# A causal convolution and an RWKV channel mix on one core: dummy matmuls and mu's transpose ahead of the convolution

## Chip, cores and metric

One NeuronCore of a Trainium2 chip. The metric is the device time of one execution in microseconds (us); a median is over several executions. Some of the numbers come from one execution that was profiled.

## What is computed

`x` is 8 x 4160 x 192, in float32. A depthwise causal convolution with 7 taps runs along the sequence, with one softmaxed row of taps for each of 8 heads of 24 channels. Its result goes through a channel mix in the manner of RWKV, which blends each token with its predecessor by `mu_k` and `mu_r`:

```python
w = softmax(weight)                       # 8 x 7
y[b, s] = sum_k w[h, k] * x[b, s - 6 + k] # per channel, h is its head
y_prev  = y shifted by one token (zero ahead of the first)
xk = mu_k * y + (1 - mu_k) * y_prev
xr = mu_r * y + (1 - mu_r) * y_prev
k  = relu(xk @ w_k)                       # 192 -> 1024
v  = (k * k) @ w_v                        # 1024 -> 192
out = sigmoid(xr @ w_r) * v
```

## The kernel before

TensorE (PE in the profile) does the convolution as matmuls with banded 128 x 128 matrices (`toe`, one for each head), and then the three products. The batch is taken in four pairs; a pair's tokens are cut into groups for the convolution and into steps of 512 tokens (the first has 256) for the channel mix. A step is cut into slots, each of which fills one PSUM tile of 128 x 1024 with `ps_k`. A slot runs on PE (`k_mm`, L592), then through ReLU on ScalarE (`k_relu`, ACT, L604), then squared on VectorE (`k_square`, DVE, L618). Four slots make a bundle, and the order of all work is written out by hand: each engine runs its instructions strictly in the order of the program text (`tc.manual_schedule`), bundle by bundle, with tables that say which step's blend, convolution or output goes into which bundle.

The change is in what runs ahead of the first bundles. `prologue` (L825) does this:

- SP and ACT issue the loads of the taps and of group 0's `x` (`x_f`, in float32); SP then issues two small loads of `mu_raw` (L176), 1.5 KB each, the last ones on its queue for the next 25 us. POOL issues the load of group 1's `x` (`xb`), makes masks, and issues the loads of `w_k` in two halves (L225), then more of `x`, `w_r` and `w_v`.
- PE first runs dummies that nobody reads: `SHORT` = 85 matmuls of one column (L852), then `WARM[0]` = 3 of 512 columns (`warm`, L823). They need only `ones_t` and `zeros`. Then come, in `softmax` (L240), eight small matmuls that spread the taps over the partitions (L253); they wait for VectorE's `w_tap` (L251). Then `WARM[1]` = 2 more dummies of 512 columns, while VectorE builds `toe` from the taps (`make_toe`, L295) and ACT casts group 0's `x` (L246).

`bundle_first` (L870) then convolves groups 0 and 1, three blocks of 64 channels each. For a block, `conv_t` (L402, matmuls at L412) writes a PSUM tile, ACT casts it to `yT` (`to_yT`, L422), and for group 0 VectorE forms the difference of neighbours (`diff`, L535) and blends it (`mix`, L548) into `xk`. The blend needs `mu` as one value per partition: `turn_mu` (L281) transposes `mu_raw` on PE into the dummies' PSUM tile `warm_ps`, and VectorE copies it from there (L882). The transpose stands behind the first block of the convolution:

```python
for n, (g, c) in enumerate((g, c) for g in range(2) for c in range(NC)):
    o = tiles[n % 2][:, n // 2 % 2, :]
    conv_t(g, c, o, range(groups[g][2]))
    if n == 0:
        turn_mu()
    to_yT(g, c, o, 0, groups[g][2], nc.scalar.copy)
```

Group 0 has 3 blocks of time for each channel block, so 3 x 24 matmuls; group 1 has 4, so 3 x 32. Behind them `bundle_first` runs the four slots of step 0, with the blend of step 1 on VectorE beside them.

Of the kernel before, what the change touches and what calls it, by code (L numbers as in the profile page):

```python
# [14 lines left out]
def kernel(  # L15
# [11 lines left out]
    nc = tc.nc  # L27
# [5 lines left out]
    P = 128  # L33
# [13 lines left out]
    NPAIR = B // 2  # L47
    YC = 16
    WARM = (3, 2)
    SHORT = 85  # L50

    const = ctx.enter_context(tc.tile_pool(name="const", bufs=1))
    two = ctx.enter_context(tc.tile_pool(name="two", bufs=2))
# [25 lines left out]
    n = 0  # L79
# [34 lines left out]
    def x_tile(g):  # L114
        p, base, nb, _, on_pe = groups[g]
        first = g if g in sparse else (0, 4, 6)[(g > 3) + (g > 5)]
        if g == first:
            homes[g] = two.tile([P, TG, 2, D], BF16, tag="xb", name="xb")
        n0 = sum(grp[2] for grp in groups[first:g])
        xb = homes[first][:, n0 : n0 + nb, :, :]  # L120
        xbs[g] = xb
        if g > 4:

            nc.vector.memset(xb[0:1, 0, 0, 0:2], 0.0)  # L124
        if base == 0 and g > 0:
            nc.gpsimd.memset(xb[0:32, 0, :, :], 0.0)  # L126
        if on_pe is False and base + 2 * nb * HB > S:
            n0 = nb - (base + 2 * nb * HB - S) // HB - 1
            nc.gpsimd.memset(xb[Q:P, n0:nb, :, :], 0.0)

    def load_x(g, batches=range(2)):
        p, base, nb, _, on_pe = groups[g]
        xb = xbs[g]
        if on_pe:
            parts, step, rows = ((0, base),), BLK, P
        elif g in sparse:
            parts, step, rows = [(32 * i, base + i * nb * TB) for i in range(4)], TB, 32
        else:
            parts, step, rows = ((0, base), (Q, base + nb * HB)), HB, Q
        for s in batches:  # L140
            b = 2 * p + s
            for q0, start in parts:
                lo, hi = 0, nb
                t0 = start - HALO
                if t0 < 0:
                    lo = 1
                    nc.gpsimd.dma_start(out=xb[HALO:rows, 0, s, :], in_=x[b, 0 : rows - HALO, :])
                while t0 + (hi - 1) * step + HALO + step > S:
                    hi -= 1
                    r0 = t0 + hi * step  # L150
                    if r0 + HALO < S:
                        nc.gpsimd.dma_start(out=xb[q0 : q0 + S - r0, hi, s, :], in_=x[b, r0:S, :])
                nc.gpsimd.dma_start(  # L153
                    out=xb[q0 : q0 + rows, lo:hi, s, :],
                    in_=bass.AP(
                        tensor=x.tensor,
                        offset=x.offset + (b * S + t0 + lo * step) * D,
                        ap=[[D, rows], [step * D, hi - lo], [1, D]],
                    ),
                )  # L160

    def load_x_first(eng, q0, q1, n0, n1, s0, s1):

        rows = [[D, q1 - q0]]
        rest = [[BLK * D, n1 - n0]] if n1 - n0 > 1 else [[S * D, s1 - s0]]
        eng.dma_start(
            out=x_f32[q0:q1, n0:n1, s0, :] if n1 - n0 > 1 else x_f32[q0:q1, n0, s0:s1, :],
            in_=bass.AP(
                tensor=x.tensor,
                offset=x.offset + (s0 * S + n0 * BLK - HALO + q0) * D,  # L170
                ap=rows + rest + [[1, D]],
            ),
        )

    def load_mu(i, m):
        nc.sync.dma_start(  # L176
            out=mu_raw[i * NC : (i + 1) * NC, :].rearrange("c (s q) -> c s q", s=2),
            in_=bass.AP(tensor=m.tensor, offset=m.offset, ap=[[Q, NC], [0, 2], [1, Q]]),
        )

    place = three.tile([P, NF * STEP], FP32, tag="k2", name="x_f32")
    n = groups[0][2] * 2 * D
# [5 lines left out]
    zeros = const.tile([P, BANK], BF16)  # L188
    ones_t = const.tile([P, P], BF16)
# [9 lines left out]
    warm_ps = ring.tile([P, 2, BANK], FP32, tag="k", name="warm")  # L199
# [34 lines left out]
    def load_wr():  # L234
        load_thirds(wr, moe_w_r, D)
# [21 lines left out]
    def masks_tap():  # L257

        nc.gpsimd.affine_select(
            out=tap8.rearrange("p (c r) -> p c r", r=8),  # L260
            in_=ones_t[0:8, 0:8].unsqueeze(1).to_broadcast([8, P // 8 + 1, 8]),
            pattern=[[0, P // 8 + 1], [-1, 8]],
            compare_op=ALU.is_equal,
            fill=0.0,
            base=0,
            channel_multiplier=1,
        )

    def select_equal(t, n):
        nc.gpsimd.affine_select(  # L270
            out=t,
            in_=(ones_t if t is ident else ones6)[0:n, 0:n],
            pattern=[[1, n]],
            compare_op=ALU.is_equal,
            fill=0.0,
            base=0,
            channel_multiplier=-1,
        )

    def turn_mu():  # L280
        nc.tensor.transpose(out=warm_ps[:, 1, 0 : 2 * NC], in_=mu_raw, identity=ident6)  # L281

    def masks_band():
        nc.gpsimd.affine_select(
            out=band, in_=ones_t, pattern=[[-1, P]], compare_op=ALU.is_ge, fill=0.0, base=0, channel_multiplier=1
        )
        nc.gpsimd.affine_select(
            out=band, in_=band, pattern=[[1, P]], compare_op=ALU.is_ge, fill=0.0, base=K - 1, channel_multiplier=-1
        )

    def make_toe():

        for h0, h1 in ((0, 3), (3, 6), (6, H)):
            n = h1 - h0
            nc.vector.tensor_tensor(  # L295
                out=toe[:, h0:h1, :].rearrange("p h (c r) -> p h c r", r=8),
                in0=w_per[:, h0:h1, :].unsqueeze(2).to_broadcast([P, n, P // 8, 8]),
                in1=band.rearrange("p (c r) -> p c r", r=8).unsqueeze(1).to_broadcast([P, n, P // 8, 8]),
                op=ALU.mult,
            )  # L300
# [520 lines left out]
    def warm(ps, n):  # L821
        for i in range(n):
            nc.tensor.matmul(out=ps[:, i % 2, :], lhsT=ones_t, rhs=zeros, start=True, stop=True)  # L823

    def prologue():  # L825
        nc.sync.dma_start(
            out=w_raw,
            in_=weight,
        )
        nc.vector.memset(x_f32[0:32, 0, :, :], 0.0)  # L830
        nc.vector.memset(ones_t, 1.0)
        for st, eng in ((0, nc.scalar), (1, nc.sync)):
            load_x_first(eng, 0, P, 1, groups[0][2], st, st + 1)
        load_x_first(nc.scalar, 16, P, 0, 1, 0, 2)
        load_x_first(nc.sync, HALO, 16, 0, 1, 0, 2)
        load_mu(0, moe_mu_k)
        load_mu(1, moe_mu_r)
        nc.scalar.preload_act_table(AF.Exp)
        nc.vector.memset(zeros, 0.0)
        nc.vector.memset(w_nrm, 0.0)  # L840
        nc.vector.memset(ones6, 1.0)
        x_tile(0)
        x_tile(1)
        load_x(1)
        masks_tap()
        select_equal(ident6, 2 * NC)
        masks_band()
        load_wk(0, DF // 2)

        for i in range(SHORT):  # L850
            q = slice(i % 4 * 32, i % 4 * 32 + 32)
            nc.tensor.matmul(  # L852
                out=warm_ps[q, 0, 0:1], lhsT=ones_t[:, 0:32], rhs=ones_t[:, 0:1], start=True, stop=True
            )
        warm(warm_ps, WARM[0])
        x_tile(2)
        softmax()
        warm(warm_ps, WARM[1])
        make_toe()
        load_wk(DF // 2, DF)  # L860
        load_x(2)
        select_equal(ident, P)
        x_tile(3)
        load_x(3)
        load_wr()
        load_wv()
        x_tile(4)
        load_x(4)

    def bundle_first(ns):  # L870
        new_yT(0)
        tiles = [ring.tile([P, 2, BANK], FP32, tag="k", name="ps_t") for _ in range(2)]
        for n, (g, c) in enumerate((g, c) for g in range(2) for c in range(NC)):
            o = tiles[n % 2][:, n // 2 % 2, :]
            conv_t(g, c, o, range(groups[g][2]))
            if n == 0:
                turn_mu()
            to_yT(g, c, o, 0, groups[g][2], nc.scalar.copy)
            if g == 0:
                diff(0, slice(c, c + 1))  # L880
                if c == 0:
                    nc.vector.tensor_copy(out=mu.rearrange("p i c -> p (i c)"), in_=warm_ps[:, 1, 0 : 2 * NC])  # L882
                mix(0, 0, slice(c, c + 1))

        diff(1, slice(0, 1))
        mix(1, 0, slice(0, 1))
        for n in ns[:2]:
            k_mm(n)
            k_relu(n)
        diff(1, slice(1, 3))  # L890
        scale(1, 0, 1, 2)
        add_y(1, 0, slice(1, 3))
        for n in ns[2:]:
            k_mm(n)
            k_relu(n)
        for n in ns:
            k_square(n)
        run(late, 0)
# [166 lines left out]
```

## Time and profile before

| | us |
|---|---|
| median of three timed runs | 411.61 |
| lowest, highest of them | 411.23, 412.36 |
| the profiled execution | 410.53 |
| its span, first to last instruction | 408.80 |
| busy in the span: PE, VectorE, ScalarE, POOL | 400.9, 370.9, 354.6, 57.6 |
| convolution's first matmul (L412) | 5.56 after the span's start |
| mu's transpose (L281) | 6.29 |
| first matmul of the channel mix (L592) | 10.12 |
| first ReLU (L604) | 11.69 |

The span is what the profile shows; the time of the execution has 1.73 us around it. PE and PEld are TensorE's matmuls and weight loads, which overlap. The page states for groups of instructions how long one takes and what ended the idle time before it; the timeline lists the instructions in order, merged where they follow one another. Times of the early stage are counted from the start of the span.

### The profile page before, as it was taken

How to read it: one execution, taken by the hardware profiler on the slowest of the kernel's cores; microseconds unless marked ns; L12 is line 12 of the kernel's file. 1: busy time of each engine (PE TensorE's matmuls, PEld its weight loads, DVE VectorE, ACT ScalarE, POOL GpSimd, SP SyncE). 2: the span in 40 equal slices, each digit the busy share in tenths (PEclk: the TensorE clock that was granted, in tenths of full speed). 3: DMA queues.
4: the chain of work that ended last, by engine and by line, in shares of the span. 5: the costliest groups of instructions: out<-in, count | busy, mean ns of one | idle time of the engine just before them, and what ended most of it. 6: DMA issues, size and time to landing. Idle time of an engine off the chain costs nothing.

```text
span 408.8 us, 17415 instructions
## 1 busy us (share of the span) xinstructions
PE 400.9 (98%) x7670; PEld 302.1 (74%) x7670; DVE 370.9 (91%) x672; ACT 354.6 (87%) x426; POOL 57.6 (14%) x91
## 2 busy tenths in 40 slices
PE   7899999999999999999999999999999999999996
PEld 4567767777867777777777777777777778777795
DVE  5999899998989999989999899999999899999973
ACT  6899988898998889988898998889899877877781
POOL 8732022030060004004020022000000000000000
PEclk9999999999999999999999999999999999999999
DMA  9999889996779978989995997977523856221223
GB/s 150 185 200 227 181 182 219 240 203 181 152 109 221 238 201 128 218 219 180 197 167 128 217 196 128 165 190 199 127 79 92 197 145 159 79 73 48 80 79 117
DMA packets 139124, 66.35 MB, mean 162 GB/s; under 512 B 89365, under 2 KB 139049, under 8 KB 139049
## 3 DMA queue, kind: packets, MB, share of 16 engines
q1 hardware_dynamic: 95704, 48.32, 46.8%
q0 software_dynamic: 42544, 16.36, 34.6%
q8 instruction: 60, 0.98, 1.0%
q10 hardware_dynamic: 800, 0.57, 0.5%
q14 instruction: 16, 0.12, 0.1%
HBM read 33.29 MB, written 36.99 MB: 172 GB/s over the span
## 4 chain that ended last, share of the span: by engine, by line
PE 91%; DMA 1%; SPq 1%; ACT 1%; issue 0%; DVE 0%; ACTq 0%
PE ps_v L680 40%; PE ps_k L592 39%; PE ps_r L649 8%; PE ps_c L363 2%; PE ps_v L632 1%; DMA y_dram<-y 1%; PE ps_c L318 1%; SPq L465 1%; ACT k_sb L604 1%; ACT y L336 0%; ACT y L438 0%; PE ps_c L392 0%; DVE o_sb L716 0%; ACTq L400 0%; ACTq L336 0%
## 5 line engine op out<-in xcount | busy, mean ns | idle before, releaser
L604 ACT ACTIVATE k_sb<-ps_k 128x1024 bf16<-128x1024 f32 x260 | 253.3, 1038 | 33.5 <-PE ps_k L592 32.8
L618 DVE TENSOR_TENSOR k<-k_sb 128x1024 bf16<-128x1024 bf16 x260 | 173.3, 686 | 25.4 <-ACT k_sb L604 25.3
L592 PE MATMUL ps_k<-xk,wk 64*128 64x512 bf16 (+1 forms) x1632 | 191.9, 367 | 1.2 <-DMA wk<-in_moe_w_k_dram 1.1
L680 PE MATMUL ps_v<-wv,k 64*128 64x192 bf16 x4032 | 188.4, 243 | 0.1
L680 PEld LDWEIGHTS <-k 64*128 64x128 bf16 x4032 | 168.4, 94 | 12.5 <-issue 4.8
L592 PEld LDWEIGHTS <-wk 64*128 64x128 bf16 x1632 | 83.3, 94 | 56.7 <-DMA wk<-in_moe_w_k_dram 1.6
L153 POOL DMA_DIRECT2D xb<-in_x_dram x62 | 44.0, 717 | 142.1 <-DVE xb L124 58.9
L696 DVE TENSOR_TENSOR o_sb<-ps_v,r_sb 128x768 f32<-128x768 f32 x64 | 60.8, 950 | 2.6 <-issue 2.4
L660 ACT ACTIVATE r_sb<-ps_r 128x768 bf16<-128x768 f32 x65 | 53.6, 827 | 8.7 <-PE ps_v L680 7.2
L336 ACT CAST y<-ps_c 128x960 bf16<-128x960 f32 (+2 forms) x84 | 52.7, 707 | 0.2 <-DMA y_dram<-y 0.2
L649 PEld LDWEIGHTS <-xr 64*128 64x128 bf16 x780 | 34.9, 94 | 14.1
L649 PE MATMUL ps_r<-wr,xr 64*128 64x192 bf16 x780 | 43.2, 243 | 0.0
L566 DVE TENSOR_SCALAR xr<-d,mu 128x512 bf16<-128x512 bf16 (+1 forms) x102 | 35.0, 347 | 0.0
L566 DVE TENSOR_SCALAR xk<-d,mu 128x512 bf16<-128x512 bf16 (+1 forms) x99 | 32.8, 360 | 0.1
L535 DVE TENSOR_TENSOR d<-yT 128x1536 bf16<-128x1536 bf16 (+4 forms) x36 | 31.2, 868 | 1.0 <-ACT yT L422 0.8
L572 DVE TENSOR_TENSOR xr<-xr,yT 128x1536 bf16<-128x1536 bf16 (+1 forms) x33 | 31.1, 941 | 1.1
L572 DVE TENSOR_TENSOR xk<-xk,yT 128x1536 bf16<-128x1536 bf16 (+3 forms) x33 | 30.4, 922 | 0.1
L519 POOL COPY y_tail<-yT 128x195 bf16<-128x195 bf16 x4 | 2.7, 673 | 90.2 <-DMA yT<-y_dram 90.2
L363 PEld LDWEIGHTS <-toe 32*32 32x32 bf16 x640 | 4.4, 87 | 8.6 <-issue 7.4
L363 PE MATMUL ps_c<-xb,toe 32*32 32x240 bf16 x640 | 9.3, 267 | 0.0
L126 POOL MEMSET xb<- 32x384 bf16 x3 | 1.2, 408 | 55.3 <-DVE xb L124 55.3
L412 PEld LDWEIGHTS <-xb 128*32 128x32 bf16 (+3 forms) x264 | 4.4, 104 | 2.7 <-issue 1.3
(58 smaller groups left out, 65.1 us busy)
## 6 DMA issues: line engine op xcount, KB each, us to landing
out_dram<-o_sb SPq DMA_DIRECT2D x128, 192.0 KB
xb<-in_x_dram POOLq DMA_DIRECT2D x52, 240.0 KB, 8.1
y_dram<-y SPq DMA_DIRECT2D x40, 195.0 KB
y_dram<-y SPq DMA_DIRECT2D x16, 210.0 KB
xb<-in_x_dram POOLq DMA_DIRECT2D x4, 228.0 KB, 4.5
xb<-in_x_dram POOLq DMA_DIRECT2D x4, 192.0 KB, 6.7
wk<-in_moe_w_k_dram POOLq DMA_DIRECT2D x4, 192.0 KB, 6.1
xb<-in_x_dram POOLq DMA_DIRECT2D x2, 216.0 KB, 5.2
```

Of the source, the lines that this page charges most:

```text
L153: nc.gpsimd.dma_start(out=xb[q0 : q0 + rows, lo:hi, s, :], in_=bass.AP(tensor=x.tensor, offset=x.offset + (b * S + t0 + lo * step) * D, ap ...
L336: nc.scalar.copy(out=bass.AP(tensor=y.tensor, offset=y.offset + d, ap=[y.ap[0], [m * 2 * D, 2], [2 * D, m], [Q, 2], [1, b - a]],), in_=bas ...
L535: nc.vector.tensor_tensor(out=shaped(s, diffs[s][:, cs, :L]), in0=y_of(s, cs, 1), in1=y_of(s, cs, 0), op=ALU.subtract)
L566: nc.vector.tensor_scalar(out=t[:, c, :L], in0=diffs[s][:, c, :L], scalar1=mu[:, i, c : c + 1], scalar2=None, op0=ALU.mult)
L572: nc.vector.tensor_tensor(out=o, in0=o, in1=y_of(s, sl, 0), op=ALU.add)
L592: nc.tensor.matmul(out=ps[:, i, f * L : (f + 1) * L], lhsT=wk[r, c, fs], rhs=xk[r, c, :L], start=c == 0 and f == 0, stop=c == NC - 1 and f ...
L604: nc.scalar.activation(out=k_sb, in_=ps.rearrange("p a b -> p (a b)"), func=AF.Relu)
L618: nc.vector.tensor_tensor(out=o, in0=i, in1=i, op=ALU.mult)
L649: nc.tensor.matmul(out=ps[:, i, k * D : (k + 1) * D], lhsT=xr[q, c, ts], rhs=wr[q, c, :], start=c == 0, stop=c == NC - 1,)
L660: nc.scalar.activation(out=r_sbs[s, j], in_=r_ps.pop((s, j))[:, :, 0 : 2 * D], func=AF.Sigmoid)
L680: nc.tensor.matmul(out=v_ps[s, j][:, bank, k * D : (k + 1) * D], lhsT=k2s[s][q, f, t * P : (t + 1) * P], rhs=wv[q, f, :], start=half == 0 ...
L696: nc.vector.tensor_tensor(out=o_sb.rearrange("p (b t) d -> p b (t d)", b=2), in0=v_ps.pop((s, j)), in1=r_sbs.pop((s, j)), op=ALU.mult,)
```

## The change

A new helper `fill` issues dummy matmuls of 128 columns into the first bank of `warm_ps`. Six of them follow the first three long dummies, in front of the tap matmuls. `turn_mu` moves out of `bundle_first` to behind the last two long dummies, in front of the whole convolution, and three more short fills follow it. Nine one-column dummies are dropped, so that PE has as many instructions as before.

```diff
     WARM = (3, 2)
-    SHORT = 85
+    SHORT = 76
+    FILL = (6, 3)
...
+    def fill(n):
+        for i in range(n):
+            nc.tensor.matmul(out=warm_ps[:, 0, 0:P], lhsT=ones_t, rhs=zeros[:, 0:P], start=True, stop=True)
+
     def prologue():
...
         warm(warm_ps, WARM[0])
+        fill(FILL[0])
         x_tile(2)
         softmax()
         warm(warm_ps, WARM[1])
+        turn_mu()
+        fill(FILL[1])
         make_toe()
...
             conv_t(g, c, o, range(groups[g][2]))
-            if n == 0:
-                turn_mu()
             to_yT(g, c, o, 0, groups[g][2], nc.scalar.copy)
```

## The prediction

> **What bounds the kernel now.** I read the page first, then the chain of waits, then the first 16 us in order of time, because the diff touches nothing later. The page gives PE 98% of the span. From about 29 us to the end the chain of waits is PE work with hardly a gap, so whatever moves the end must move PE's start into that stretch. The question is whether anything ahead of the convolution (L412) does so. The timeline, whose columns are start, duration, engine, line, operation, and in brackets the idle time ahead of it with its releaser:
>
> ```profile
> 3.98 0.20 DVE L251 STREAM_TRANSPOSE w_tap<-w_nrm 32x32 bf16<-32x32 bf16 x1
> 4.23 0.36 PE L253 MATMUL w_ps<-w_tap,tap 8*128 8x8 bf16 x8 [0.48 <-DVE w_tap L251]
> 4.53 1.03 PE L823 MATMUL warm<-zeros,ones_t 128*128 128x512 bf16 x2
> 5.56 0.79 PE L412 MATMUL ps_t<-toe,xb 128*32 128x120 bf16 x24
> 6.29 0.27 PE L281 MATMUL warm<-ident,mu_raw 6*128 6x6 f32 x1
> 6.41 0.46 ACT L422 CAST yT<-ps_t 128x360 bf16<-128x360 f32 x1
> 6.48 1.64 PE L412 MATMUL ps_t<-toe,xb 128*32 128x120 bf16 x50
> ...
> 8.34 1.02 PE L412 MATMUL ps_t<-toe,xb 128*32 128x120 bf16 x62 [0.22 <-DMA xb<-in_x_dram]
> ...
> 8.96 0.48 DVE L548 SCALAR_TENSOR_TENSOR xk<-d,mu,yT 128x256 bf16<-128x256 bf16 x1
> ...
> 10.12 0.28 PE L592 MATMUL ps_k<-xk,wk 64*128 64x256 bf16 x1
> ...
> 10.83 1.48 PE L592 MATMUL ps_k<-xk,wk 64*128 64x256 bf16 x24 [0.43 <-DMA wk<-in_moe_w_k_dram]
> ...
> 12.36 0.69 DVE L572 TENSOR_TENSOR xk<-xk,yT 128x1024 bf16<-128x1024 bf16 x1
> ...
> 13.01 2.77 PE L592 MATMUL ps_k<-xk,wk 64*128 64x256 bf16 x35 [0.69 <-DMA wk<-in_moe_w_k_dram]
> ...
> 14.93 0.69 DVE L618 TENSOR_TENSOR k<-k_sb 128x1024 bf16<-128x1024 bf16 x1 [0.57 <-ACT k_sb L604]
> ...
> 15.84 0.69 DVE L618 TENSOR_TENSOR k<-k_sb 128x1024 bf16<-128x1024 bf16 x1 [0.22 <-ACT k_sb L604]
> ```
>
> Three transfers pace the start: PE reaches group 1 of the convolution and waits for xb until 8.34, reaches the first FFN slot at 10.12 and waits for wk until 10.83, and waits for wk's second half until 13.01. All are issued by POOL, which waits for nothing that PE does here. Behind wk, ACT's ReLUs run from 11.69 to 18.66 with one hole of 0.24 us. So PE work that ends sooner before 10 us ends in front of a closed door.
>
> The matmul durations, as minimum, median, maximum in ns with first and last start, show the clock, which the page's PEclk row (nines throughout) does not; and the mu transpose has a semaphore wait of its own on PE's queue:
>
> ```profile
> L412 PE MATMUL ps_t<-toe,xb x264: 213/216/308, 5.6 to 17.9; 128*32 128x120 bf16 x67, 128*16 128x120 bf16 x24, 128*24 128x120 bf16 x23, 128*8 128x120 bf16 x18
> ```
>
> ```profile
> L281 PEldq EVENT_SEMAPHORE  x1: 51/51/51, 6.2 to 6.2; - x1
> L281 PE MATMUL warm<-ident,mu_raw x1: 266/266/266, 6.3 to 6.3; 6*128 6x6 f32 x1
> ```
>
> One by one in the trace, the matmuls of L412 take 279 to 308 ns and four go out per 100 ns up to 7.57; from 8.34 they take 216 ns at four per 52.5 ns. The clock doubled between 7.84 and 8.34 us.
>
> [...] the trace's 512-column dummies start 427 ns apart (2.697 and 3.124)[...]. [...]
>
> **Part by part.**
> *Nine short dummies fewer.* The 85 go out from 1.535 to 2.195, 7.9 ns apart: 9 x 7.9 = 0.07 us earlier for the long dummies. Nothing waits for those but PE itself, which then waits for w_tap: 0.
> *fill(6).* Cold, 128 columns are a quarter of 427, 107 ns: 6 x 107 = 0.64 us, from 3.48 (3.55 less 0.07) to 4.12. w_tap ends at 4.18 and the tap matmuls start at 4.23. It fits, with 0.1 us to spare; bounds 0 and, if a dummy drags its weight load (0.1 us each at most), +0.5 on the taps, which toe passes on. I take 0. [...]
> *turn_mu moved.* It issues no DMA and passes no queue but PE's. It takes 0.20 us of PE (6.287 to the next start, 6.483), 0 net since it only moves. But it waits for mu_raw. The completion marks of the mu_r load, read in the trace's raw records, are at 5.46, 5.62 and 6.12, and the transpose starts 0.17 us after the last; the convolution's matmul before it started at 6.05. So today the transpose is already held by that load, by about 0.1 us. Moved ahead, it stands in PE's queue from about 5.0 (warm) or 5.3 (cold), and all of the convolution is queued behind it; ACT's casts of ps_t (L422) wait for that, and VectorE for them. If mu lands as before: transpose at 6.29, fill(3) from 6.48 (3 x 107 = 0.32 cold; at half, 0.16 warm), convolution at 6.64 warm or 6.80 cold instead of 5.56. If mu lands by 5.3 the delay is only 0.20 + 0.16 to 0.32 less the present gap of 0.2: 0.15 to 0.3. I take the late landing.
> *Where the delay goes.* Group 0 has 72 matmuls. Warm at 13.1 ns: 6.64 + 0.95 = 7.6, ahead of the 7.67 of today. Cold at 25 ns with the switch at 8.1: 52 by then, 20 more by 8.36. Both meet xb at 8.34. VectorE's chain for xk of step 0 ends at 9.44 today. Its head, the first L412 third, ends later by 1.24 cold and by 1.24 − 0.16 (fills) − 24 x 12 ns (0.29, the first third at full clock) = 0.8 warm. So xk is whole at 10.2 warm or 10.7 cold, and its last third is needed at about 11.2, after wk's 10.83: hidden, by 0.5 at least. VectorE had 0.13 idle before the next step, so it is 0.67 warm or 1.1 cold late there: xk of step 1 at 13.7 or 14.2 instead of 13.05; PE needs it after 12 pairs of 0.109 from 13.01, 14.3: hidden, by 0.1 in the cold case. Then the two idle times before L618, 0.57 + 0.22 = 0.79, take the rest: 0 warm, 0.3 cold.
> *Sum.* 0 warm; cold up to +0.3, of which VectorE's later holes take some more. Without the cover of wk the warm case would cost 0.7. Against the profiled execution, 410.53 (span 408.80 plus 1.73 around it), that is 410.53 to 410.8. The median of the three timed runs is 1.08 higher, so I predict 411.61 + 0 = **411.6**.
>
> **The rivals.**
> *A: the usual execution starts colder than the profiled one, and the change mends that.* For it: [...] 410.53 lies below all three timed runs (411.23 to 412.36). If the switch came only after slots 0 and 1, their 12 pairs would take about 0.107 more each, 1.28 us; ACT's one hole of 0.24 takes little of it, so 1.0 to 1.3 reach ReLU's unbroken row. Ended in all executions: 411.61 − 1.3 = 410.3. [...]
> *B: slower, by mu's wait.* The hole from 5.3 to 6.29, 1.0 us of idle array, is larger than the one that fill(6) closes[...]. [...] group 0 ends at 8.6 and group 1 (96 x 25 ns) at 11.0; the FFN's first slots run cold: 0.2 of late start and 12 pairs x 0.107 = 1.28, less 0.24, give +1.25, so 412.9. It decides from the point where the clock comes after about 12 us[...]. For it: the completion mark at 6.12. [...]
> *C: the fills bring no clock at all but mu's wait is short.* Then everything is as today, at 411.6 to 411.9; it ends inside the forecast's own bound.
>
> **How the numbers follow.** A measurement of this kernel can tell about 0.3% (1.23 us) from no change, so "same" is 410.38 to 412.84. The forecast with C: 0.58, all same, 411.3 to 411.9 but for scatter of some 0.4 between medians (the three runs span 1.1). A: 0.26, most of it under 410.4; B: 0.16, at 412.1 to 412.9 or beyond, most of it over. I put faster 0.24, same 0.62, slower 0.14. The range takes in A's 410.3 and goes toward B: 410.3 to 412.7.
>
> **What would show it.** L412's durations at 216 ns from the first on, and 128-column dummies 54 ns apart in the second pause, show the early clock; 308 ns up to 8 us or later refute it. The transpose of L281 starting at about 6.3 with PE idle from 5.0 on shows mu's wait; a start near 5.2 refutes it. xb at 8.34 and wk at 10.83 and 13.0 unchanged, with the first ReLU at 11.7, show that the transfers cover it all. The prediction is wrong if wk's transfers land earlier or later than now, if the ReLU row starts later than 11.9, or if the timed executions differ from the profiled one by their clock.

## The result and the profile after

The changed kernel takes 416.28 us (median of 6 runs, 415.09 to 417.34) against 411.42 for the kernel before (6 runs, 410.10 to 412.52): ratio 1.0113, 95% interval 1.0087 to 1.0140. It is slower by 4.9 us. The profiled execution took 416.32 us, with a span of 414.6.

The timeline of the changed kernel's PE from 6 us on; all lines of code stand a little lower (L282 is the transpose, L413 the convolution, L593 the first product, L828 the fill):

```profile
6.21 0.24 PE L282 MATMUL warm<-ident,mu_raw 6*128 6x6 f32 x1 [0.61 <-DMA mu_raw<-in_moe_mu_r_dram]
6.38 0.50 PE L828 MATMUL warm<-zeros,ones_t 128*128 128x128 bf16 x3
6.81 3.38 PE L413 MATMUL ps_t<-toe,xb 128*32 128x120 bf16 x123
13.33 1.33 PE L413 MATMUL ps_t<-toe,xb 128*32 128x120 bf16 x45 [3.15 <-issue]
14.59 1.68 PE L593 MATMUL ps_k<-xk,wk 64*128 64x256 bf16 x14
```

The mu wait is there, as forecast, and the convolution starts at 6.81 instead of 5.56. What the prediction didn't have is the fourth line: PE stops in the middle of a block of group 1, after 123 of its 168 matmuls, and stands still for 3.15 us with the releaser "issue", which means that the profile shows nothing that it waited for. Its waits up to 30 us say it again (us in total, times, longest):

```profile
PE ps_t L413 <- issue: 3.1, 1, 3.1
...
PE warm L282 <- DMA mu_raw<-in_moe_mu_r_dram: 0.6, 1, 0.6
```

What came meanwhile is in the DMA view. The queues of the kernel before, from 4 to 6 us (packets, MB, share of the 16 engines, which passes 100% where the times of packets overlap):

```profile
q0 software_dynamic: 713, 0.27, 122.3%
q8 instruction: 1, 0.02, 2.9%
q1 hardware_dynamic: 32, 0.01, 2.4%
q10 hardware_dynamic: 11, 0.01, 0.9%
```

The same stretch of the changed kernel, and then its 10 to 13.3 us:

```profile
q0 software_dynamic: 765, 0.29, 126.3%
q1 hardware_dynamic: 65, 0.03, 5.9%
q10 hardware_dynamic: 55, 0.03, 5.4%
```

```profile
q0 software_dynamic: 1121, 0.61, 136.3%
q8 instruction: 1, 0.02, 1.8%
```

The page gives q8 and q14 the kind "instruction". It has these rows for the whole of the kernel before, and q8's counts are the same in the changed one:

```profile
q8 instruction: 60, 0.98, 1.0%
q14 instruction: 16, 0.12, 0.1%
```

PE has 7,670 matmuls and as many weight loads on the page, and 0.98 MB over 15,340 is 64 bytes for each; the other engines together run some 2,000 instructions, which at that size fits q14's 0.12 MB. By these counts q8 carries PE's instructions: each of its 60 packets is 16 KB in the trace's records, at 64 bytes 256 instructions. **The first of them starts at 4.91 us in the kernel before and at 11.06 in the changed one.** In the trace PE had started 448 instructions (444 weight loads and matmuls, two at its start and two waits for semaphores) when it stopped at 9.94, and it went on at 13.33, 2.27 us after the packet's start. In the kernel before, with the packet at 4.91, PE started its 449th instruction at 8.93 without such a stop.

**Where the 5.8 us of the two profiled spans lie.** The 123rd matmul of the convolution starts 0.97 us later than before (9.94 against 8.98): mu's wait and a cold clock. Then PE stands from 9.94 to 13.33, 3.39 us. The remaining stretches to the first ReLU take 0.05 longer in sum, so that the ReLU row starts at 16.09 instead of 11.69, 4.40 later. Instruction for instruction, PE is 4.21 us behind at 27 us and stays there up to 119 us. By 134 us it is 4.75, by 210 us 5.86, and 5.81 at the end; the last large step is one more stop without a visible reason:

```profile
208.98 0.31 PE L364 MATMUL ps_c<-xb,toe 32*32 32x240 bf16 x11 [0.87 <-issue]
```

Here, too, a q8 packet started 2.6 us before (206.40). One such stop also stands in the profile of a kernel below that loses nothing in all (a_short79, at 243.8 us, with its packet 2.2 us before), which suggests that the later ones belong to the scatter of this kernel and not to the change; that isn't shown.

The clock follows the stop: behind it the trace's clock record has half speed from 13.39 to 16.81 us, and matmuls of L413 take up to 308 ns again. Before 10 us the changed kernel's matmuls of L413 took 279 to 308 ns in 118 of 123 cases, so cold (73 of the first 123 in the kernel before), and the clock record has the first grant of full speed at 9.98, when PE had just stopped. Three stretches of 1 us of the changed kernel follow, each with its length, the busy time of PE, PEld, VectorE, ScalarE and POOL with their instructions, then the granted clock, the DMA share and GB/s; the clock goes from 1.00 to 0.50:

```profile
13.00:14.00 1.00, 0.67 (x32) 0.67 (x35) 0.00 (x0) 0.10 (x1) 0.23 (x2) 0.70 1.58 189
14.00:15.00 1.00, 1.00 (x31) 0.68 (x24) 0.00 (x0) 0.76 (x2) 0.84 (x2) 0.50 1.59 188
15.00:16.00 1.00, 1.00 (x12) 0.76 (x10) 0.69 (x1) 0.25 (x1) 0.71 (x2) 0.50 1.60 191
```

### The profile page after: what moved, and what is told of

It is laid out like the page before. It is cut to its first block, busy times and chain, and to the rows that moved or that the text cites. A ratio compares the mean times of both kernels' runs of the same rounds, so it can differ in the third digit from the quotient of the medians.

```text
span 414.6 us, 17414 instructions
## 1 busy us (share of the span) xinstructions
PE 403.4 (97%) x7669; PEld 305.0 (74%) x7670; DVE 370.6 (89%) x672; ACT 354.8 (86%) x426; POOL 57.2 (14%) x91
## 4 chain that ended last, share of the span: by engine, by line
PE 92%; ACT 1%; issue 1%; DVE 0%; ACTq 0%
PE ps_v L681 41%; PE ps_k L593 39%; PE ps_r L650 8%; PE ps_c L364 2%; PE ps_v L633 1%; PE ps_c L319 1%; ACT k_sb L605 1%; ACT y L439 0%; PE ps_c L393 0%; DVE o_sb L717 0%; ACTq L401 0%; ACTq L605 0%
## 5 line engine op out<-in xcount | busy, mean ns | idle before, releaser
L593 PE MATMUL ps_k<-xk,wk 64*128 64x512 bf16 (+1 forms) x1632 | 192.5, 368 | 0.3 <-ACT k_sb L605 0.3
L593 PEld LDWEIGHTS <-wk 64*128 64x128 bf16 x1632 | 84.3, 95 | 55.4 <-issue 1.3
L413 PE MATMUL ps_t<-toe,xb 128*32 128x120 bf16 (+3 forms) x264 | 6.3, 271 | 3.1 <-issue 3.1
```

Source lines behind the costliest of these rows:

```text
L593: nc.tensor.matmul(out=ps[:, i, f * L : (f + 1) * L], lhsT=wk[r, c, fs], rhs=xk[r, c, :L], start=c == 0 and f == 0, stop=c == NC - 1 and f ...
```

## The experiments

The first theory, F, a guess: PE asks for its next block of instructions on passing a certain instruction; mu's wait holds it short of that, and the request then queues behind POOL's loads. The rival, M: mu's wait and the cold clock cost the time by themselves. In what follows "fetch" is the start of the first 16 KB packet on q8, from one profiled execution of each kernel; the medians are over all runs. Instructions are counted in PE's own program, a weight load and a matmul being two.

### Three dummies more, and the parts alone

```diff
-    SHORT = 76
+    SHORT = 79          # a_short79: the changed kernel
...
-    SHORT = 85
+    SHORT = 76          # b_short76: the kernel before
```

> The changed kernel with three more one-column dummies (79), so that six more PE instructions stand ahead of mu's transpose, 196 instead of 190; all else is as changed. Theory F (instruction fetch: PE asks for its next block of instructions on passing about instruction 192 to 197; in the changed kernel it stands at number 191, waiting for mu, until 6.2 us, and then the fetch queues behind POOL's loads until 11): the first 16 KB fetch goes out near 5 us as before, no stall of PE inside group 1 of the convolution, 411 to 412 us. Theory M (mu's wait and the cold clock cost the time by themselves): mu still waits until 6.2, so 416 us as changed.

> The kernel before with 76 one-column dummies instead of 85 and nothing else: no fills, mu's transpose in its old place. Theory F: 18 instructions fewer stand ahead of the convolution, so the same instruction number is passed only after the convolution's start at 5.5 us, about 0.8 us later than before; the first fetch then comes behind POOL's loads, at 8 us or later, and if after 9 PE stalls in group 1: 412 to 416 us. Theory M: no difference, 411.4 us.

```diff
         warm(warm_ps, WARM[1])
-        turn_mu()
         fill(FILL[1])       # a_mu_back: the changed kernel
...
             conv_t(g, c, o, range(groups[g][2]))
+            if n == 0:
+                turn_mu()
```

> The changed kernel with mu's transpose put back behind the convolution's first block; the nine fills and the 76 short dummies stay. Theory F: nothing holds PE ahead of instruction 197, as in the kernel before; first fetch near 5 us, no stall, 411 to 412 us. Theory M: mu's wait is gone too, so the same, 411 to 412 us. A theory that the fills themselves cost the time: 415 us or more.

```diff
+        load_mu(0, moe_mu_k)
+        load_mu(1, moe_mu_r)
         nc.vector.memset(x_f32[0:32, 0, :, :], 0.0)   # a_mu_first: the changed kernel
...
         load_x_first(nc.sync, HALO, 16, 0, 1, 0, 2)
-        load_mu(0, moe_mu_k)
-        load_mu(1, moe_mu_r)
```

> The changed kernel with SP's two loads of mu issued straight after the taps' load, ahead of the loads of x; the transpose stays ahead of the convolution. Mu should land by 4 us, so that the transpose waits for nothing. Theory F: first fetch near 5 us, no stall; 411 to 412 us, or 411.0 if the fills bring the clock early. Theory M: mu's wait is gone, 411 to 412 us as well. If it stays at 416, both are wrong and the place of the transpose or the fills cost the time in another way.

| | median us | ratio to before, interval | fetch, us |
|---|---|---|---|
| a_short79 | 411.32 | 0.9995 (0.9981 to 1.0008) | 4.98 |
| b_short76 | 411.03 | 0.9990 (0.9976 to 1.0004) | 6.74 |
| a_mu_back | 411.61 | 1.0006 (0.9983 to 1.0029) | 6.42 |
| a_mu_first | 412.12 | 1.0004 (0.9989 to 1.0020) | 7.55 |

Three one-column dummies, 24 ns of PE at 7.9 ns from one to the next, take the whole loss away, while mu's wait stays. The waits of a_short79 up to 30 us:

```profile
...
PE ps_k L593 <- DMA wk<-in_moe_w_k_dram: 1.3, 1, 1.3
PE ps_t L413 <- DMA xb<-in_x_dram: 0.5, 1, 0.5
PE ps_t L413 <- ACT yT L423: 0.5, 2, 0.2
PE warm L282 <- DMA mu_raw<-in_moe_mu_r_dram: 0.2, 1, 0.2
```

There is no "issue" on PE; the longest are for transfers, as in the kernel before. That speaks against M, and a_short94 below, which has mu's wait and a cold clock as long as the changed kernel's, refutes it. F is in trouble too: b_short76, which by F should ask late and lose, loses nothing, and in a_mu_back and a_mu_first the fetch comes at 6.42 and 7.55 us and not near 5. Each part alone is free in time; the loss needs both.

### How sharp the step is

`SHORT = 77` and `SHORT = 78` in the changed kernel, and, for the pair without any fill, the kernel before with `SHORT = 76` and `turn_mu()` moved to behind `warm(warm_ps, WARM[1])`:

> The changed kernel with one more short dummy: 192 PE instructions ahead of mu's transpose. Theory F, now with a place: the request falls at one instruction between the 191st (the changed kernel, which is held there) and the 196th (79 short dummies, which is not). If at the 192nd or earlier, fetch near 5 us and 411.4; if later, fetch behind POOL's loads at 7 to 11 us, and with a stall in group 1 416. A graded theory (each dummy earns its own share of time) would give about 414.5.

> The changed kernel with two more short dummies: 194 PE instructions ahead of mu's transpose. Theory F: either 411.4 with the fetch near 5 us or as changed (416, or an unlucky mean between where the fetch is late by less), and a step between 76 and 79, not a slope. The graded theory: about 413.

> The kernel before with 76 short dummies and mu's transpose ahead of the convolution, without any fill. 178 instructions stand ahead of the transpose, so the request point lies in the convolution's first block, behind mu's wait: passed at about 6.5 us. Theory F with a queue that is busy from there on: late fetch, stall in group 1, 414 to 416. If the fills are a needed part of the loss: 411 to 412. The 76 dummies alone gave 411.0 with a fetch at 6.7 us, so a request some tenths of a us later tells how sharp the edge is.

a_short77 takes 414.78 us, ratio 1.0075 (1.0041 to 1.0109), fetch 10.71. a_short78: 415.39, 1.0068 (1.0040 to 1.0096), fetch 8.94. b_mu_early76: 415.98, 1.0086 (1.0058 to 1.0114), fetch 10.91. All lose, and 79 doesn't: a step, not a slope. The fills are no part of it, since b_mu_early76 has none. PE's line of b_mu_early76 behind its stop, the same 3 us:

```profile
13.22 1.08 PE L412 MATMUL ps_t<-toe,xb 128*8 128x120 bf16 x36 [3.06 <-issue]
```

In all eight kernels, here and below, with a fetch at 8.9 us or later PE stops after 448 started instructions and goes on 2.3 to 2.5 us after the fetch's start; in a_short78 it stops 1.46 us only, since its fetch came at 8.94 (that execution took 412.88 us, the lowest of its seven).

### Does the fetch queue behind POOL's loads?

Both kernels with POOL's loads of w_k and everything behind them held back:

```diff
+    def rest():
+        nc.vector.memset(wk[:, :, 0:2], 0.0)
+        nc.vector.memset(wk[:, :, DF // 2 : DF // 2 + 2], 0.0)
+        load_wk(0, DF // 2)
...
                 diff(0, slice(c, c + 1))
+                if c == 0:
+                    rest()
```

> The changed kernel with POOL's loads of w_k and all that follow them held until VectorE has formed the first difference (about 8.3 us), by two small memsets of wk there; PE's order is as changed, so the request for instructions is as late as in the changed kernel (about 6.3 us). Theory F with the fetch queueing behind POOL's loads: the fetch starts by 7.6 us, when group 1's load of x has ended, and PE doesn't stall inside group 1's convolution; the time itself is about 4 us worse than the kernel before, since w_k comes 4 us later, so only the fetch and the stall count. If the fetch is late by itself: again 10 to 11 us, and the stall stays.

> The kernel before with POOL's loads of w_k and all after them held as in the run a_pool_late. It prices that hold alone: w_k about 4 us later, so 415.5 to 417.5. If the changed kernel under the same hold costs no more than this one, the change costs nothing once its fetch is served at once; if it costs 4 to 5 us more, the loss isn't in the fetch.

a_pool_late: 417.59 us, 1.0140 (1.0118 to 1.0163), from two runs; b_pool_late: 416.40, 1.0103 (1.0071 to 1.0134), from four. The fetch of a_pool_late starts at 7.51, just behind the last landing mark of group 1's load of x (7.31), and its convolution runs through; its PE waits for w_k instead:

```profile
PE ps_k L593 <- DMA wk<-in_moe_w_k_dram: 3.6, 3, 1.7
```

Under the hold the change costs 1.2 us and not 4.9, and two runs don't place that more closely. With the fetch at 7.51 and not at 11.06, POOL's loads are part of what makes it late. They aren't all of it: b_pool_late, under the same hold, has its fetch at 4.16. How the fetch takes its turn beside those loads is not shown: with them on the queues, the changed kernel's first one comes 5 us after mu, but no view shows when PE asks for it.

### Is it the count ahead of the transpose?

79 dummies put 196 instructions ahead of the transpose. So does the changed kernel with two lines swapped; three more kernels put dummies of one column between the last long ones and the transpose:

```diff
-        turn_mu()
         fill(FILL[1])
+        turn_mu()           # a_fill_first
...
+        for i in range(4):  # a_late4; 8 and 16 in a_late8, a_late16
+            q = slice(i % 4 * 32, i % 4 * 32 + 32)
+            nc.tensor.matmul(
+                out=warm_ps[q, 0, 0:1], lhsT=ones_t[:, 0:32], rhs=ones_t[:, 0:1], start=True, stop=True
+            )
         turn_mu()
```

> The changed kernel with its last three fills put ahead of mu's transpose instead of behind it: the same instructions and the same 76 short dummies, but 196 of them ahead of the transpose. Theory F (request at the 195th or 196th instruction): the fetch starts near 5 us, no stall, 411.4 us as the kernel before, and the transpose still waits for mu. If the step between 78 and 79 short dummies came from the dummies' own time and not from the count, it stays at 415 to 416.

> The changed kernel with four one-column dummies put between the last long dummies and mu's transpose; 76 short ones at the start as changed. 198 instructions ahead of the transpose, but the tap matmuls, the first instructions that wait, stand where they do in the changed kernel. Theory F2 (PE's front end asks for the next block at a fixed instruction; [...] with 79 dummies the point is read already while the taps wait): the point lies behind the 196th, so this may be just short of it: 415, or 411.5 if the point is the 197th or 198th. Theory S (the start's 79 short dummies are what counts, whatever stands ahead of the transpose): 415.

> As a_late4 with eight: 206 instructions ahead of the transpose. Theory F2: [...] 411.5 here and a fetch between 5 and 6.7 us. Theory S: 415, fetch at 9 us or later.

> As a_late4 with sixteen: 222 instructions ahead of the transpose. Theory F2: 411.5, fetch between 5 and 6.7 us. Theory S: 415. If all three of these runs are slow, a late point isn't what mu's wait holds up, and the count ahead of the transpose has no part in it.

| instructions ahead of the transpose | of the taps' first | median us | ratio, interval | fetch |
|---|---|---|---|---|
| a_fill_first, 196 | 170 | 415.20 | 1.0071 (1.0044 to 1.0097) | 9.68 |
| a_late4, 198 | 170 | 415.85 | 1.0095 (1.0062 to 1.0127) | 11.13 |
| a_late8, 206 | 170 | 415.61 | 1.0077 (1.0044 to 1.0111) | 9.78 |
| a_late16, 222 | 170 | 414.70 | 1.0060 (1.0026 to 1.0095) | 11.40 |

All lose in the median, though not in each execution (one of a_late16's six took 411.46). So F as I had put it falls, and so does its second form, F2. What divides the kernels whose early transpose waits for mu, with all of POOL's loads, is the count ahead of the **tap matmuls**, which wait for VectorE until 4.2 us, the first wait on PE since the dummies began: 158, 170, 172 and 174 lose, 176 and 206 (a_short94, below) don't. 176 is what the kernel before has there.

### The wait or the place?

```diff
-        nc.tensor.transpose(out=warm_ps[:, 1, 0 : 2 * NC], in_=mu_raw, identity=ident6)
+        nc.tensor.transpose(out=warm_ps[:, 1, 0 : 2 * NC], in_=ones6_wide, identity=ident6)   # a_no_mu_wait
...
-    SHORT = 76
+    SHORT = 94          # a_short94
```

> The changed kernel with mu's transpose reading a tile of ones set by VectorE instead of mu_raw: the transpose stands where the change puts it, with 190 instructions ahead, but waits for no load. The blend then uses ones for mu, so mu is left out of the result. Theory H (both are needed, too few instructions ahead of the tap matmuls and a wait for mu's load ahead of the convolution): fetch by 7.5 us, no stall, 411 to 412. If the place of the transpose is enough without its wait: fetch at 9 us or later, 415.

> The changed kernel with 94 short dummies, 226 instructions ahead of mu's transpose and 208 ahead of the tap matmuls, where mu still waits: the whole change with more than enough in front. Theory H: fetch at 5 us or earlier, no stall, 411.4 as the kernel before, also with the early clock; if the early clock or an earlier fetch is worth anything beyond that, 410.5.

a_no_mu_wait, which leaves mu out of its result, takes 411.77 us, ratio 1.0001 (0.9980 to 1.0022), fetch 6.64. a_short94, with 206 instructions ahead of the taps (the expectation says 208), takes 411.43, 0.9985 (0.9973 to 0.9998), fetch 5.14. So it is the wait and not the place; and with enough instructions in front, the whole change, wait included, costs nothing. The PE timeline of a_short94 shows how much the transfers do hide:

```profile
6.24 0.24 PE L282 MATMUL warm<-ident,mu_raw 6*128 6x6 f32 x1 [0.48 <-DMA mu_raw<-in_moe_mu_r_dram]
6.41 0.50 PE L828 MATMUL warm<-zeros,ones_t 128*128 128x128 bf16 x3
6.84 4.27 PE L413 MATMUL ps_t<-toe,xb 128*32 128x120 bf16 x168
11.04 1.59 PE L593 MATMUL ps_k<-xk,wk 64*128 64x256 bf16 x25
13.26 2.78 PE L593 MATMUL ps_k<-xk,wk 64*128 64x256 bf16 x35 [0.63 <-DMA wk<-in_moe_w_k_dram]
```

Mu's wait, the convolution's start at 6.84 and a cold clock up to 10.25 are all as in the changed kernel, 0.9 us late at L593; but the convolution runs through, the wait for w_k's second half takes the delay up, and the span is 408.9, that of the kernel before within 0.1. As a version, a_short94 is at most 0.3% better than the kernel before.

**What stays open.** Shown is that in the eight kernels where 158 to 174 instructions stand ahead of the tap matmuls' wait, mu's wait comes next and POOL's loads are there, the first fetch comes at 8.94 us or later in its profile and PE stands still for 1.46 to 4.36 us. Few instructions alone put it at 6.42 to 7.55 (b_short76, a_mu_back, a_mu_first, a_no_mu_wait), which is soon enough; mu's wait alone leaves it at about 5 (a_short79, a_short94).

Why is not shown, but the landing marks of POOL's loads fit a simple reading: that with few instructions in front PE asks for the block only after the wait at which it stands, and that the fetch then waits behind the loads that POOL has issued by then.

| wait ends (semaphore record for mu) | last load that POOL has issued by then | its landing marks | fetch |
|---|---|---|---|
| taps, 4.2 (the four kernels named) | x of group 1, its second transfer, by 3.0 | 6.3 to 8.3 | 6.42 to 7.55 |
| mu, 5.95 (a_pool_late) | the same | 6.6 to 7.3 | 7.51 |
| mu, 5.64 to 5.98 (a_late8, a_short78, a_fill_first) | second of w_k's four transfers, by 5.5 | 8.7 to 11.6 | 8.94 to 9.78 |
| mu, 6.10 to 6.56 (the changed kernel and the other four) | third of w_k's four transfers, by 6.1 | 10.0 to 13.1 | 10.71 to 11.40 |

With 176 or more in front, the block would be asked for before the taps' wait. Ten of the thirteen fetches start between the marks of their own execution, the other three within 0.2 us of them. But the marks of neighbouring transfers overlap, within a group the order of the waits isn't that of the fetches, and each row rests on one execution of each kernel, so this is a reading that fits and not a proof.

## Why the prediction was wrong, point by point

- **Where the delay goes: right.** The step said that a convolution that starts 1.2 us late, cold, is hidden by xb and by w_k's halves. a_short94 does just that, with w_k alone as the cover. b_short76 points the same way: it starts 0.56 us late, its clock rises only at 12.2 us in its profile, and it takes 411.03 us.
- **turn_mu moved: right in its wait, wrong in its reach.** The transpose started at 6.21 and the convolution at 6.81, as worked out for the cold case (6.29 and 6.80). But the step said that it "issues no DMA and passes no queue but PE's", and took everything queued behind it to be PE's own work. By the page's counts PE's instructions come on a queue of their own, q8 (60 packets, 0.98 MB). With the wait moved, the first fetch on it started at 11.06 instead of 4.91 us, and PE stood still for 3.15 us; without the wait at the same place (a_no_mu_wait) the fetch started at 6.64 and nothing was lost. This is the step that failed, together with the next:
- **Nine short dummies fewer, costed at 0: wrong.** The two edits lose only together. The nine dummies' 0.07 us are indeed nothing; their 18 instructions, of which the six fills gave 12 back ahead of the taps, are what decides. That the change leaves PE's total count as it was says nothing on the count ahead of one wait.
- **fill(6): right in time, unsure in its purpose.** The tap matmuls started at 4.25 against 4.23. The early clock was a guess and isn't shown to follow from the fills: with all nine of them in place, full speed came at 9.98 in the changed kernel's profile, at 5.50 in a_short79, 6.02 in a_no_mu_wait, 10.25 in a_short94, against 8.1 before. It is no use in any of them, since what starts sooner waits for xb and w_k (0.5 and 1.3 us in a_short79): a_mu_back has the fills without mu's wait, its profile has full speed at 6.04, and it takes 411.61 us.
- **Rival A, a colder usual execution: refuted.** Profiled executions in which the clock rises at 5.5 us (a_short79), at 12.2 (b_short76) and at 13.7 (a_mu_first) took 411.49, 410.76 and 412.02 us, all within the scatter of the kernel before (410.0 to 413.2 in 39 executions taken beside them).
- **Rival B, slower by mu's wait: right in the wait and the sign, wrong in the mechanism and the size.** It had cold FFN slots, up to +1.25 us. The cold clock came second here: PE was at half speed from 13.4 to 16.8, after it had stood still. With the stop taken away (a_short79, a_short94) nothing of B is left.
- **Rival C, no early clock but a short wait: half of it.** The changed kernel's profile has no early clock, but the wait is as long as the forecast's late landing.

The profile of the kernel before held a hint that the prediction passed over: the row "q8 instruction" with 60 packets, and its first packet between 4 and 6 us in the DMA view, ahead of the landing of w_k.

## What to carry to other kernels

Ahead of a stretch with heavy DMA traffic, look at where the instruction packets fall, and compare them before and after an edit, as one would with a data load: here PE had started 448 instructions by 9.94 us and then stood still for 3.15 us, with its packet at 11.06 instead of 4.91. The wait that was moved forward held back the packet too, to 11.06 from the 6.64 of a_no_mu_wait, and two nearly free instructions more or less ahead of an earlier wait decided it, 174 (a_short78, 8.94) against 176 (a_short79, 4.98). A stop with the releaser "issue" in the middle of a uniform run of matmuls, with a packet on the instruction queue some 2 us before its end (2.3 to 2.5 in the eight kernels), is the mark to look for.

## What the runs showed of the hardware

- PE stopped after 448 started instructions in each of the eight kernels whose first 16 KB block came at 8.9 us or later, and went on 2.3 to 2.5 us after that packet's start, of which the packet itself takes 0.9 to 1.0. It did not stop there in the nine whose block came by 7.6 us.
- The start of that packet ranged from 4.91 us (the kernel before) to 11.40 (a_late16), by edits of a few dummies and one wait; with POOL's loads of w_k held back as well, it was 4.16 (b_pool_late) and 7.51 (a_pool_late).
- The TensorE clock rose at 5.5 us in a profiled execution of 411.49 us (a_short79) and at 13.7 in one of 412.02 (a_mu_first), and in the changed kernel it fell back to half speed for 3.4 us (13.39 to 16.81) after PE had stood still for 3.15.
